# One Strassen level on two of the four chunks of a spatial mixing matmul, with z2 stored by feature planes and the attention's output projection moved to the end

## The chip, the cores and the metric

The kernel runs on one core of one Trainium2 chip. The metric is the device time of one execution in microseconds (us). An execution is somewhat longer than the span of the profile, which begins with the first and ends with the last instruction or transfer that the profiler records.

## The reference

A token mixer over S = 2048 positions of width D = 512, all in float32. After a layer norm of `x`, two branches run and are joined:

```python
xn = _layernorm(x, axis=-1)
s = _A_ref(xn, A_wqkv, A_wo)        # 32 heads of 16; each position looks at 8 positions, 2 apart
g = _silu(_B_ref(xn, ...))
return x + s * g

# branch B
z = _gelu(jnp.einsum("bsd,df->bsf", x, w_in))
z1 = z[..., :Fh]                                   # Fh = 896
z2 = _layernorm(z[..., Fh:], axis=-1)
g = jnp.einsum("ts,bsf->btf", w_sp, z2) + b_sp[None, :, None]   # the spatial mixing, w_sp is 2048 x 2048
return jnp.einsum("bsf,fd->bsd", z1 * g, w_out)
```

The spatial mixing is the largest product: 2048 x 2048 times 2048 x 896.

## The kernel before

Every matmul operand is split in two parts, `hi` (rounded to the type fp32r that TensorE reads) and `lo` (the rest), and each product is three matmuls: hi by hi, hi by lo, lo by hi. ScalarE (ACT) makes the hi part with a copy, VectorE (DVE) makes the lo part with a subtraction (`split`, L155 and L156; with a scale for the spatial weights in `prep`, L139 and L140).

The work on TensorE (PE) stands in this order. First q, k and v for 16 tiles of 128 positions (`product`, `pair`, L344 to L364), which go to DRAM (`qkv_d`). Then z1 (L528 to L530), kept transposed, through a gelu to DRAM (`z1_d`). Then z2 (`z2_half`, L552 to L554) with its layer norm: statistics on DVE (L567, L568), small steps on GpSimd (POOL), the centred hi and lo parts by ACT and DVE (L571, L572) into the large resident buffer `BIG`. Then the spatial mixing in four chunks `c` of 512 output positions (L607 to L609): for each of 16 blocks `js` of input positions and each of 7 blocks `f` of features three matmuls of 128x512, so 336 per chunk, into 7 of the 8 PSUM banks. At the end of a chunk ACT copies the banks out (L629), DVE adds the bias (L636) and multiplies by z1 (`gated`, L585), and the result `ut` goes to DRAM (`g_d`); the last chunk stays on chip. In the end phase the projection `b` of the gated result (21 matmuls a tile) and the projection `s` of the attention (12 matmuls a tile) alternate tile by tile (`tail`, L652 to L654), then silu, product, residual and output.

The attention itself has no matmul. DVE does it (`attention`, L471 to L508) for 8 groups of heads, at the lowest priority, between DVE's other work; the outputs go to DRAM in `o_d` and come back in the end phase (`load_o`).

What sets the order: a scheduler lays all instructions of each engine in one fixed sequence before the run, with priorities from the order of the code; instructions in `pin` keep the order of the code. On the chip each engine works through its sequence in that order and waits at its head. PSUM has 8 banks in one pool (`mm`). Split weights have 8 buffers of each part (`whi`, `wlo`), loads of weights have 3 (`raw`); they are requested by SyncE's queue (SP) in the order of its sequence.

Of the kernel before, what the change touches and what calls it, by code (L numbers as in the profile page):

```python
# [16 lines left out]
P = 128  # L17
# [17 lines left out]
HALO = (W - 1) * DIL  # L35
PAD = 16
# [10 lines left out]
def kernel(  # L47
# [52 lines left out]

    def xn_at(j):
        o = (NT * 2 * (FH - D)) + j * 2 * D
        return BIG[:, o : o + D], BIG[:, o + D : o + 2 * D]

    def z2_at(j):
        o = j * 2 * FH
        return BIG[:, o : o + FH], BIG[:, o + FH : o + 2 * FH]

    def ut_at(c, f):
        o = c * 2 * FB * CT + f * 2 * CT  # L110
        return BIG[:, o : o + CT], BIG[:, o + CT : o + 2 * CT]
# [6 lines left out]

    def mm(name):
        return ps.tile([P, 512], F32, tag="mm", name=name, bufs=8)  # L120

    def fetch(src, n, name):
        raw = raws.tile([P, 512], F32, tag="raw", name=name + "r", bufs=3)
        pin(nc.sync.dma_start(raw[:, :n], src))
        return raw

    def prep(src, n, name, pool=None, scale=None, raw=None):
        if raw is None:
            raw = fetch(src, n, name)
        if pool is None:  # L130
            hi = wts.tile([P, 512], F32R, tag="whi", name=name + "h", bufs=8)
            lo = wts.tile([P, 512], F32R, tag="wlo", name=name + "l", bufs=8)
        else:
            hi = pool.tile([P, 512], F32R, tag=name + "h", name=name + "h")
            lo = pool.tile([P, 512], F32R, tag=name + "l", name=name + "l")
        if scale is None:
            split(hi[:, :n], lo[:, :n], raw[:, :n])
        else:
            nc.scalar.activation(hi[:, :n], raw[:, :n], AF.Copy, scale=scale)  # L139
            nc.vector.scalar_tensor_tensor(  # L140
                lo[:, :n], raw[:, :n], scale, hi[:, :n].bitcast(F32), op0=ALU.mult, op1=ALU.subtract
            )
        return hi, lo

    def rstd(mv):
        nc.vector.tensor_scalar(mv[:, 1:2], mv[:, 1:2], EPS, None, op0=ALU.add)
        nc.gpsimd.tensor_tensor(mv[:, 1:2], mv[:, 1:2], nhalf, op=ALU.pow)
# [6 lines left out]
    def split(hi, lo, src):  # L154
        pin(nc.scalar.activation(hi, src, AF.Copy))  # L155
        pin(nc.vector.tensor_tensor(lo, src, hi.bitcast(F32), op=ALU.subtract))  # L156

# [25 lines left out]
    def turned_x(j, xt):  # L183
        pt = mm(f"xt_{j}")
        for i in range(KB):
            pin(nc.tensor.transpose(pt[:, i * P : (i + 1) * P], xt[:, i * P : (i + 1) * P], ident))
        pin(nc.scalar.activation(xn_at(j)[0], pt, AF.Copy))
        return pt

    def low_x(j, pt):  # L190
        hi, lo = xn_at(j)
        pin(nc.vector.tensor_tensor(lo, pt, hi.bitcast(F32), op=ALU.subtract))
# [42 lines left out]
    def column_tile(j):  # L235
# [5 lines left out]
        pin(nc.scalar.activation(xn_at(j)[0], cols[j], AF.Copy))  # L241
# [10 lines left out]
    def opening(wg):  # L252
        def high(k):
            hi = wts.tile([P, 512], F32R, tag="whi", name=f"wqkv_0_{k}h", bufs=8)
            lo = wts.tile([P, 512], F32R, tag="wlo", name=f"wqkv_0_{k}l", bufs=8)
# [8 lines left out]
        def times(j, *kab):  # L264
            for k, a, b in kab:
                pin(nc.tensor.matmul(
                    first[j], xn_at(j)[a][:, k * P : (k + 1) * P], wg[k][b],
# [70 lines left out]
    def product(g, j, wg):  # L338
        xh, xl = xn_at(j)
        pq = mm(f"qkv_{g}_{j}")  # L340
        for k in range(KB):
            wh, wl = wg[k]
            c = slice(k * P, (k + 1) * P)
            nc.tensor.matmul(pq, xh[:, c], wh, start=k == 0, stop=False)  # L344
            nc.tensor.matmul(pq, xh[:, c], wl, start=False, stop=False)  # L345
            nc.tensor.matmul(pq, xl[:, c], wh, start=False, stop=k == KB - 1)  # L346
# [74 lines left out]
    for g in range(1, NG):  # L421
        for j in range(OPEN if g == 1 else 0, NT, 2):
            if g == 1 and j == NT // 2:
# [3 lines left out]
                rb = t2("rb", tag="tz", bufs=2)  # L427
# [13 lines left out]
    att = tc.tile_pool(name="att", bufs=1)  # L441
    ap_ = att.__enter__()
    NJ = 4
    at_priority = [LOW]

    def attention(sub):
# [49 lines left out]
        for j0 in range(0, NT, NJ):  # L496
# [9 lines left out]
            nc.vector.tensor_tensor(pr[:, 0], pr[:, 0], pr[:, 1], op=ALU.add)  # L506
            tt = ap_.tile([P, NJ * CS // Q, Q], F32, tag="tt", name=f"tt_{sub}_{j0}", bufs=2)
            nc.vector.transpose(tt.rearrange("p n q -> p (n q)"), pr[:, 0])  # L508
            for a in range(P // Q):
                dst = o_d[sub, j0 : j0 + NJ, :, a * Q : (a + 1) * Q]  # L510
                nc.sync.dma_start(
                    dst.rearrange("j (b c) q -> c (j b) q", c=Q), tt[a * Q : (a + 1) * Q]
# [7 lines left out]
    xall = BIG[:, NT * 2 * (FH - D) :].rearrange("p (c j a k t) -> p c a k j t", c=NC, j=JC, a=2, k=KB)  # L520
    for f in range(FB):
        wh, wl = prep(w_in1[:, f, :], KB * P, f"w1_{f}")
        for c in range(NC):
            pz = mm(f"z1_{f}_{c}")
            for k in range(KB):
                cc = slice(k * P, (k + 1) * P)
                xh, xl = xall[:, c, 0, k], xall[:, c, 1, k]
# [3 lines left out]
            zt = t2(f"z1t_{f}_{c}")  # L531
# [4 lines left out]
            nc.scalar.dma_start(z1_d[c, f], zt)  # L536
# [185 lines left out]
```

## Time and profile before

| | us |
|---|---|
| median of 3 runs (725.66 to 725.99) | 725.96 |
| the profiled execution | 725.2 |
| its span | 723.2 |
| PE busy in the span | 717.1 |
| DVE busy | 566.9 |
| ACT busy | 222.1 |
| POOL busy | 33.5 |
| DMA, share of 16 engines' span, both large queues | 39.1% and 10.9% |

Busy time is the time in which at least one instruction of the engine runs. Matmuls are pipelined: one lasts 389 ns in the profile, while the next begins long before it ends, so the distance between starts is what a matmul costs. Stages can be found by the lines named above: chunk 0 of the spatial mixing begins at about 295 us, and the end phase at about 600 us.

### The profile page before, as it was taken

Reading aid. Unit: us, or ns where it says so; the run is one execution under the profiler, and the core shown is the slowest. Engines: PE = TensorE matmul, PEld = TensorE weight load, DVE = VectorE, ACT = ScalarE, POOL = GpSimd, SP = SyncE. Lnnn points to the kernel's source line nnn. Section 1 sums busy time; section 2 is a strip of 40 time slices with the busy share of each in tenths; the row PEclk is TensorE's granted clock in tenths of the full one; section 3 lists DMA queues with packets and bytes.
Section 4 is the critical chain, followed back from the end, with each engine's and each line's share of the span. In section 5 each row is a group of like instructions: output and inputs, shape, how many; then the busy total and the mean of one; then the engine's idle time right before and its main releaser. Section 6 shows DMA issues by size and latency. Waiting matters only on the chain.

```text
span 723.2 us, 8807 instructions
## 1 busy us (share of the span) xinstructions
PE 717.1 (99%) x3224; PEld 599.1 (83%) x3224; DVE 566.9 (78%) x683; ACT 222.1 (31%) x341; POOL 33.5 (5%) x49
## 2 busy tenths in 40 slices
PE   8999999999999999999999999999999999999997
PEld 7888888888888889888888888888888888888886
DVE  6763699889989999999997999999999947432222
ACT  4443332342243345621231123111334234311210
POOL 3100000000001223300000000000000000000000
PEclk9999999999999999999999999999999999999999
DMA  8776874674562210352457334744368547523221
GB/s 283 237 203 183 296 245 125 189 247 142 185 219 67 63 59 26 95 166 71 148 149 249 130 83 130 258 150 132 92 222 276 150 125 204 161 88 118 86 73 44
DMA packets 111178, 111.55 MB, mean 154 GB/s; under 512 B 40736, under 2 KB 74784, under 8 KB 111136
## 3 DMA queue, kind: packets, MB, share of 16 engines
q1 hardware_dynamic: 79120, 85.43, 39.1%
q10 hardware_dynamic: 32016, 25.56, 10.9%
q8 instruction: 25, 0.41, 0.2%
q14 instruction: 17, 0.14, 0.1%
HBM read 77.07 MB, written 33.90 MB: 153 GB/s over the span
## 4 chain that ended last, share of the span: by engine, by line
PE 93%; DMA 3%; DVE 3%; SPq 1%; issue 0%; POOL 0%; ACT 0%; DVEq 0%
PE g L609 14%; PE g L607 14%; PE g L608 14%; PE qkv L346 4%; PE qkv L344 4%; PE qkv L345 4%; PE z L554 4%; PE z L553 4%; PE z L552 4%; PE b L654 4%; PE b L653 4%; PE z L530 4%; PE z L528 4%; PE b L652 4%; PE z L529 4%; PE s L654 2%
## 5 line engine op out<-in xcount | busy, mean ns | idle before, releaser
L471 DVE TENSOR_TENSOR pr<-k,q 128x2048 f32<-128x2048 f32 x32 | 73.2, 2287 | 1.5 <-DMA q<-qkv_d 1.1
L498 DVE TENSOR_TENSOR pv<-v,lg 128x2048 f32<-128x2048 f32 x32 | 73.3, 2289 | 0.9
L474 DVE TENSOR_REDUCE lg<-pr 128x128 f32<-128x2048 f32 x32 | 72.9, 2280 | 0.5
L666 DVE TENSOR_TENSOR sg<-s,sg 128x512 f32<-128x512 f32 (+1 forms) x17 | 11.2, 659 | 71.5 <-PE s L654 71.5
L504 DVE TENSOR_TENSOR pv<-pv 128x1024 f32<-128x1024 f32 x32 | 39.0, 1220 | 0.5
L364 ACT ACTIVATE stage<-qkv 128x512 f32<-128x512 f32 x36 | 21.4, 596 | 50.8 <-PE qkv L346 50.7
L661 ACT ACTIVATE sg<-b 128x512 f32<-128x512 f32 x16 | 9.6, 597 | 60.7 <-PE b L654 56.9
L585 DVE TENSOR_TENSOR gt<-gt,zl 128x512 f32<-128x512 f32 x28 | 18.9, 687 | 11.1 <-DMA zl<-z_d 11.1
L554 PE MATMUL z<-w_0h,BIG 128*128 128x512 f32 x64 | 25.0, 391 | 0.0
L553 PE MATMUL z<-w_0l,BIG 128*128 128x512 f32 x64 | 25.0, 391 | 0.0
L552 PE MATMUL z<-w_0h,BIG 128*128 128x512 f32 x64 | 24.9, 389 | 0.0
L155 ACT ACTIVATE BIG<-ul 128x512 fp32r<-128x512 f32 x21 | 13.2, 631 | 32.6 <-PE g L608 19.3
L505 DVE TENSOR_TENSOR pv<-pv 128x512 f32<-128x512 f32 x32 | 22.0, 688 | 0.6
L238 DVE TENSOR_TENSOR xT<-xT,mr 128x512 f32<-128x512 f32 x20 | 13.7, 687 | 10.9 <-DMA mr<-mv_d 6.1
L554 PE MATMUL z<-w_1h,BIG 128*128 128x384 f32 x64 | 21.5, 336 | 0.0
L552 PE MATMUL z<-w_1h,BIG 128*128 128x384 f32 x64 | 21.5, 335 | 0.0
L553 PE MATMUL z<-w_1l,BIG 128*128 128x384 f32 x64 | 21.4, 335 | 0.0
L569 POOL TENSOR_TENSOR nmz<-mvz,mone 128x1 f32<-128x1 f32 x16 | 10.0, 627 | 222.5 <-DVE mvz L568 219.7
L571 ACT ACTIVATE BIG<-zt,nmz 128x896 fp32r<-128x896 f32 x16 | 16.6, 1041 | 10.8 <-POOL nmz L569 10.8
L572 DVE SCALAR_TENSOR_TENSOR BIG<-zt,mvz,BIG 128x896 fp32r<-128x896 f32 x16 | 18.2, 1143 | 2.2 <-ACT BIG L571 2.0
L567 DVE BATCH_NORM_STATS2 zst<-zt 128x6 f32<-128x448 f32 x32 | 18.7, 607 | 0.4 <-ACT zt L555 0.2
L555 ACT ACTIVATE zt<-z 128x512 f32<-128x512 f32 (+1 forms) x24 | 12.6, 539 | 19.8 <-PE z L554 19.6
(396 smaller groups left out, 2113.0 us busy)
## 6 DMA issues: line engine op xcount, KB each, us to landing
qkv_d<-stage ACTq DMA_DIRECT2D x24, 512.0 KB
x<-in_x SPq DMA_DIRECT2D x32, 256.0 KB
k<-qkv_d SPq DMA_DIRECT2D x8, 960.0 KB
v<-qkv_d SPq DMA_DIRECT2D x8, 960.0 KB
z_d<-z1t ACTq DMA_DIRECT2D x28, 256.0 KB
zl<-z_d SPq DMA_DIRECT2D x28, 256.0 KB
ul<-g_d SPq DMA_DIRECT2D x21, 256.0 KB
g_d<-gt ACTq DMA_DIRECT2D x9, 512.0 KB
```

Source lines behind the costliest of these rows:

```text
L344: nc.tensor.matmul(pq, xh[:, c], wh, start=k == 0, stop=False)
L471: nc.vector.tensor_tensor(pr, taps(kw, j0), qb.unsqueeze(1).to_broadcast([P, W, NJ * CS]), op=ALU.mult)
L474: nc.vector.tensor_reduce(lg[:, :, j0 * HS : (j0 + NJ) * HS], pr.rearrange("p w (i d) -> p w i d", d=DH), axis=AX.X, op=ALU.add,)
L498: nc.vector.tensor_tensor(pr.rearrange("p w (i d) -> p w i d", d=DH), taps(vw, j0).rearrange("p w (i d) -> p w i d", d=DH), lg[:, :, j0 * ...
L504: nc.vector.tensor_tensor(pr[:, 0:4], pr[:, 0:4], pr[:, 4:8], op=ALU.add)
L552: nc.tensor.matmul(pz, xh[:, c], wh, start=k == 0, stop=False)
L553: nc.tensor.matmul(pz, xh[:, c], wl, start=False, stop=False)
L554: nc.tensor.matmul(pz, xl[:, c], wh, start=False, stop=k == KB - 1)
L607: nc.tensor.matmul(pg[f], zh[:, ff], wh, start=js == 0, stop=False)
L608: nc.tensor.matmul(pg[f], zh[:, ff], wl, start=False, stop=False)
L609: nc.tensor.matmul(pg[f], zl[:, ff], wh, start=False, stop=js == NT - 1)
L654: nc.tensor.matmul(pp[:, cols], lo, wh, start=False, stop=k == n - 1)
```

## The change

**Products.** Chunks 2 and 3 are mixed directly as before, and first. Chunks 0 and 1 together form a two by two block product: the output positions are the two chunks, the input positions the two halves of 8 blocks, and of the 7 feature blocks six are taken as two halves of three. One level of Strassen's method (the form with 7 products and shared sums) does these: seven block products of 8 position blocks by 3 feature blocks, so 7 x 8 x 3 x 3 = 504 matmuls. The odd feature block (`ODD`, number 3) is mixed directly: 2 x 16 x 3 = 96 matmuls. Together 600 where the two chunks had 672. Each product is a call of `block_product` (p1, p2, q6, q7, q5, q3, q4).

**Sums.** The sums of weight blocks (`block_sums`, four subtractions or additions of 128x512 for each of 8 blocks) are made by DVE from the loaded weights and stored in DRAM (`sums_d`), during z1 and the direct chunks. The sums of z2 blocks (`combine`, four of 128x384 for each of 8 pairs of tiles) are made by DVE in the z2 stage and stored (`t_d`); they come back in pairs (`operand`) into the place of feature blocks 4 to 6 in `BIG`, are split there, and are replaced four times (T2, T3, T1, T4). The products are combined by `minus` on DVE, and a product that follows into the same bank adds onto it.

**Bias and evictions.** ACT writes the bias into a PSUM bank (`seed`) and the matmuls add to it, for six blocks of chunk 3 and for the products p1 and q7 and the odd blocks. Where the bank was seeded, DVE multiplies by z1 straight from the bank; in chunk 2 and for the first block of chunk 3 DVE adds the bias from the bank into a buffer first. ACT copies no bank of the direct chunks any more.

**z2.** `BIG` is laid out by feature planes (`planes`). The variance is now applied to z2 itself and no longer to the spatial weights: GpSimd takes four small steps a tile in place of two, ACT normalises (`z2_normal`) and then splits. The tiles are made in pairs (i, 8 + i).

**Tail.** All 16 tiles of `b` come first and are stored (`b_d`), then all 16 of `s`; in the last stage `b`, `x` and the attention's tiles come back in pairs of tiles, paced by dependencies on splits (`fetch_pair`), and the output leaves in pairs. `o_d` is laid out so that loads and stores have longer rows.

**Buffers.** A pool of 8 wide buffers `t4` takes the place of several small ones, PSUM banks and weight buffers are taken in a fixed turn, and there are 4 `raw` buffers.

```diff
-    for c in range(NC):
-        pg = [mm(f"g_{c}_{f}") for f in range(FB)]
-        for js in range(NT):
-            wh, wl = prep(w_sp[c, js], CT, f"wsp_{c}_{js}", scale=mvz[:, js, 1:2])
...
-            if c < NC - 1:
-                nc.scalar.activation(gt, pg[f], AF.Copy)
...
+    def seed(key, name, src, scale=1.0):
+        banks[key] = mm(name)
+        nc.scalar.activation(banks[key], src, AF.Copy, scale=scale)
+        seeds.add(key)
+
+    for c in (2, 3):
+        for n, js in enumerate(order):
+            w = spatial.get((c, js)) or spatial_block(c, js)
             for f in range(FB):
...
+                if (c, f) not in seeds:
+                    gt = gts[:, f - f0]
+                    nc.vector.tensor_tensor(gt, src, bb[:, c - 2], op=ALU.add)
+                    src = gt
+                nc.vector.tensor_tensor(zt, src, zt, op=ALU.mult)
+                if c == 2 and f < FB - 1:
+                    seed((3, f + 1), f"g_3_{f + 1}", bb[:, 1])
...
+    def block_product(name, key, z, w, odd=None, start=True, steps=()):
+        for n, s0 in enumerate(range(0, HT, 2)):
+            pair_ = [(s, prep(w(s), CT, f"{name}_{s}")) for s in (s0, s0 + 1)]
+            for f in range(3):
+                for s, wp in pair_:
+                    three(
+                        banks[key, f], z(s, f), wp, start and s == 0, s == HT - 1, not start
+                    )
+            if odd:
+                for s, wp in pair_:
+                    three(banks["o", odd[0]], odd[1](s), wp, False, s == HT - 1, True)
+            for do in steps[n] if steps else ():
+                do()
...
+    def block_sums(i):
...
+        for out_, a, b in (
+            (low[:, 1], top[:, 1], low[:, 1]),
+            (top[:, 1], top[:, 0], top[:, 1]),
+            (top[:, 0], top[:, 0], low[:, 1]),
+            (low[:, 0], top[:, 0], low[:, 0]),
+        ):
+            nc.vector.tensor_tensor(out_, a, b, op=ALU.add)
...
+    rows_of = [c * JC + jj for c in (0, 2, 3, 1) for jj in range(JC)]
+    groups = [rows_of[i] // NJ for i in range(0, NT, NJ)]
+    fetched = {0: fetch_pair(0)}
+    os_ = [load_o(groups[0], k, slots[2, 0] + k) for k in range(KB)]
+    fetched[2] = fetch_pair(2, arrived[groups[0]])
```

Three places show how instructions move. In the rows stand the line, the operation, output <- inputs, and the size; buffer numbers follow the names.

**First place: PE where the second direct chunk begins.** Before, on PE, from the last matmuls of chunk 0 (bank g_6) to chunk 1 (banks g_0, g_1); `wsp_0h` is the hi part of the weights of position block 0:

```order
L608 MATMUL g_6_2890<-wsp_15l,BIG 128x512
L609 MATMUL g_6_2890<-wsp_15h,BIG 128x512
L607 MATMUL g_0_3365<-wsp_0h,BIG 128x512
L608 MATMUL g_0_3365<-wsp_0l,BIG 128x512
L609 MATMUL g_0_3365<-wsp_0h,BIG 128x512
L607 MATMUL g_0_3365<-wsp_1h,BIG 128x512
L607 MATMUL g_1_3366<-wsp_0h,BIG 128x512
```

With the change, from chunk 2 to chunk 3 (two rows before these also write g_0):

```order
L695 MATMUL g_0_3245<-wsp_0h,BIG 128x512
L695 MATMUL g_0_3245<-wsp_8h,BIG 128x512
L695 MATMUL g_0_3245<-wsp_8l,BIG 128x512
L695 MATMUL g_0_3245<-wsp_8h,BIG 128x512
L695 MATMUL g_0_3245<-wsp_1h,BIG 128x512
L695 MATMUL g_0_3245<-wsp_1l,BIG 128x512
L695 MATMUL g_0_3245<-wsp_1h,BIG 128x512
L695 MATMUL g_0_3245<-wsp_9h,BIG 128x512
L695 MATMUL g_0_3245<-wsp_9l,BIG 128x512
L695 MATMUL g_0_3245<-wsp_9h,BIG 128x512
L695 MATMUL g_1_3460<-wsp_0h,BIG 128x512
```

Before, 4 matmuls of the free bank g_0 stood ahead of the first one that needs a bank of the chunk before; now 12 do.

**Second place: who empties those banks.** Before, on ACT, the copies stand in one row behind the splits of weights:

```order
L139 ACTIVATE wsp_5h<-wsp_5r,mvz 128x512
L139 ACTIVATE wsp_6h<-wsp_6r,mvz 128x512
L629 ACTIVATE gt_0_3325<-g_0_2884 128x512
L629 ACTIVATE gt_0_3325<-g_1_2885 128x512
L629 ACTIVATE gt_2_3328<-g_2_2886 128x512
L629 ACTIVATE gt_2_3328<-g_3_2887 128x512
L629 ACTIVATE gt_4_3331<-g_4_2888 128x512
L629 ACTIVATE gt_4_3331<-g_5_2889 128x512
```

With the change, on DVE, at the end of chunk 2 (L739 empties a bank, L741 multiplies by z1, L184 splits a weight, L503 and L506 are attention):

```order
L503 TENSOR_TENSOR pr_4_1460<-k_1451,q_1450 128x2048
L506 TENSOR_REDUCE lg_1456<-pr_4_1460 128x8x16
L739 TENSOR_TENSOR gt_0_3457<-g_0_2987,bb_2985 128x512
L184 TENSOR_TENSOR wsp_3l<-wsp_3r,wsp_3h 128x512
L739 TENSOR_TENSOR gt_0_3457<-g_1_2988,bb_2985 128x512
L503 TENSOR_TENSOR pr_8_1463<-k_1451,q_1450 128x2048
L739 TENSOR_TENSOR gt_2_3469<-g_2_2989,bb_2985 128x512
L741 TENSOR_TENSOR zl_0_3455<-gt_0_3457,zl_0_3455 128x512
L739 TENSOR_TENSOR gt_2_3469<-g_3_2990,bb_2985 128x512
L739 TENSOR_TENSOR gt_4_3481<-g_4_2991,bb_2985 128x512
```

The emptying of the banks has moved from ACT to DVE, and attention stands between the evictions.

**Third place: SP in the last stage.** Before, on SP, in the middle of the end phase (`ol` attention, `x` residual, `out` results; tile by tile):

```order
L668 DMA out<-sg_5133 128x512
L659 DMA x_6_5327<-in_x 128x512
L591 DMA ol_5347<-o_d 64x4x128
L591 DMA ol_5396<-o_d 64x4x128
L668 DMA out<-sg_5182 128x512
```

With the change, around the start of `s` (`sg` is `b` coming back, `tt` an attention output that is stored):

```order
L548 DMA o_d<-tt_12_1732 32x2x128 x4
L932 DMA sg_5616<-b_d 128x1024
L933 DMA x_4_5617<-in_x 128x1024
L932 DMA sg_5651<-b_d 128x1024
L678 DMA ol_0_5784<-o_d 64x512 x2
L933 DMA x_6_5652<-in_x 128x1024
L678 DMA ol_3_5707<-o_d 64x512
L678 DMA ol_1_5791<-o_d 64x512
L971 DMA out<-sg_5560 128x1024
```

The transfers of a tile, spread over 33 matmuls of `b` and `s` before, have moved behind the attention's last store and beside the 12 matmuls a tile of `s`, in pieces twice as large, and `b` itself has joined them.

More of the change, by code (lines that the diff above doesn't have):

```diff
@@ L541 @@
         (k, h): prep(w_in2[:, k, HALF[h]], WID[h], f"w2_{k}_{h}")
+        for h in range(2)
         for k in range(KB)
-        for h in range(2)
     }
@@ new lines, in upper, with lower, turned, fresh @@
+    def upper(s, f):
+        return z2_block(s, f)
+    def lower(s, f):
+        return z2_block(HT + s, f)
+    def turned(s, f):
+        return z2_block(s, FB - 3 + f)
+    def fresh(key, name):
+        for f in range(3):
+            banks[key, f] = mm(f"{name}_{f}")
+    def odd_upper(s):
+        return z2_block(s, ODD)
+    def odd_lower(s):
+        return z2_block(HT + s, ODD)
+    def gated(c, f, src, zt):
+        nc.vector.tensor_tensor(zt, src, zt, op=ALU.mult)
+        split(*ut_at(c, f), zt)
@@ new lines @@
+    T1, T2, T3, T4 = [[later(operand, i, h, s0) for s0 in range(0, HT, 2)] for i, h in ((0, 0), (1, 1), (1, 0), (0, 1))]
+    block_product("p1", "p", upper, lambda s: w_sp[0, s], (0, odd_upper), start=False)
+    ya, yb = t4("ya"), t4("yb")
+    oq = t4("oq")
+    yv, o1 = [ya[:, 0], ya[:, 1], yb[:, 0]], oq[:, 0]
+    with urgent(400):
+        for f in range(3):
+            nc.scalar.activation(yv[f], banks["p", f], AF.Copy)
+        nc.scalar.activation(o1, banks["o", 0], AF.Copy)
+    nc.vector.tensor_tensor(b01[:, 1], b01[:, 0], b01[:, 1], op=ALU.add)
@@ new lines @@
+    block_product(
+        "p2", "p", lower, lambda s: w_sp[0, HT + s], (0, odd_lower), start=False,
+        steps=([], [T2[0]], [T2[1]], [T2[2]]),
+    )
+    fresh("q", "q6")
+    block_product(
+        "q6", "q", turned, lambda s: sums_d[0, s, :, 0],
+        steps=(
+            [T2[3], later(upper_first, 0)],
+            [T3[0], later(upper_first, 2)],
+            [T3[1], later(late, 2, 0, 2)],
+            [T3[2], later(late, 2, 2, 2)],
+        ),
+    )
+    for f in range(3):
+        minus(yv[f], banks["q", f], yv[f])
@@ new lines @@
+    for f in range(3):
+        seed(("q", f), f"q7_{f}", b01[:, 1], -1.0)
+    seed(("o", 1), "o2", b01[:, 1])
+    block_product(
+        "q7", "q", turned, lambda s: sums_d[0, s, :, 1], (1, odd_upper), start=False,
+        steps=([T3[3]], [T1[0]], [T1[1]], [T1[2], later(late, 2, 4, 1)]),
+    )
+    va, vb = t4("va"), t4("vb")
+    vv = [va[:, 0], vb[:, 0], yb[:, 1]]
+    for f in range(3):
+        minus(vv[f], yv[f], banks["q", f])
+    fresh("q", "q5")
+    block_product(
+        "q5", "q", turned, lambda s: sums_d[1, s, :, 1],
+        steps=([T1[3]], [later(late, 2, 5, 2)], [], []),
+    )
@@ new lines @@
+    qv = [va[:, 1], vb[:, 1], oq[:, 1]]
+    with urgent(400):
+        for f in range(3):
+            nc.scalar.activation(qv[f], banks["q", f], AF.Copy)
+    block_product(
+        "q3", "q", lambda s, f: z2_block(HT + s, FB - 3 + f), lambda s: sums_d[1, s, :, 0], start=False,
+        steps=([T4[0], later(lower_last, 4, 2)], [T4[1], later(lower_last, 6, 1)], [T4[2]], [T4[3]]),
+    )
+    fresh("q4", "q4")
+    block_product(
+        "q4", "q4", turned, lambda s: w_sp[1, HT + s], (1, odd_lower), start=True,
+        steps=(
+            [later(upper_last, 4, 2)],
+            [later(upper_last, 6, 1)],
+            [later(late, 3, 0, 2)],
+            [later(late, 3, 2, 1)],
+        ),
+    )
@@ L647, in proj @@
+    for f in range(3):
+        banks["q", f] = banks["q4", f]
+    wout = [prep(w_out[:, f, :], D, f"wout_{f}") for f in range(FB)]
+    lower_first(0)
+    lower_first(2)
+    late(3, 3, 2)
+    late(3, 5, 2)
     def proj(n, src, w, name, cols=slice(0, D)):
```

432 lines of the change are left out of this document (284 added, 148 removed).

## Prediction

> **What bounds the kernel now.** I read the busy times first, then the waits of PE, then the chain that ended last, then the stages. Engine, busy us (share of the span) and instructions; the wait rows give who waited for whom, us in total, times, longest; the chain row gives shares of the span.
>
> ```profile
> PE 717.1 (99%) x3224; PEld 599.1 (83%) x3224; DVE 566.9 (78%) x683; ACT 222.1 (31%) x341; POOL 33.5 (5%) x49
> ...
> PEclk9999999999999999999999999999999999999999
> ```
> ```profile
> PE warm L247 <- POOL ident masks.py:199: 1.4, 1, 1.4
> PE xt L186 <- DVE mvx L171: 0.5, 1, 0.5
> PE qkv L266 <- ACT BIG L187: 0.2, 1, 0.2
> ```
> ```profile
> PE 93%; DMA 3%; DVE 3%; SPq 1%; issue 0%; POOL 0%; ACT 0%; DVEq 0%
> ```
>
> PE is busy 99% of the span at the full granted clock, its recorded waits sum to 2.1 us, all in the opening, and 93% of the chain is PE. So a matmul that goes shortens the run by its own spacing, unless a wait takes its place. The spacing comes from one group whose first instance is the first feature block of chunk 0 and whose last is the seventh of chunk 3 (duration min/median/max, first and last start):
>
> ```profile
> L607 PE MATMUL g<-wsp_7h,BIG x28: 389/389/389, 328.0 to 560.6; 128*128 128x512 f32 x28
> ```
>
> Between the two lie three chunks of 336 and 6 x 3 = 18 matmuls, 1026 in 232.6 us: **0.2267 us each**, across chunk ends too.
>
> **What the change takes from PE.** Chunks 0 and 1 took 672 matmuls and take 600; PE's sequence shrinks by the same 72. 72 x 0.2267 = 16.3 us. The profiled execution took 725.2 us (2.0 around its span, which I keep), so matmuls alone give **708.9**. The median of the runs shown is 0.8 higher, so a result may lie that much above the sum.
>
> The Trainium skill, "TensorE: Matmul & The Clock Gate", section "Back-to-back issue gap", gives about 131 ns as the sustained spacing for 512 columns. By that the 72 matmuls would be worth 9.4 us and the sum 715.8; the trace, 226.7 ns over 1026 matmuls, decides against it.
>
> **What is added, and what hides it.** The critical question is DVE, which fills its time with attention. A row of stages gives the stretch, its length, busy us (instructions) of PE, weight loads, DVE, ACT and POOL, the granted clock, the DMA share and GB/s; group rows follow.
>
> ```profile
> 371.00:524.00 153.00, 153.00 (x677) 126.73 (x676) 142.68 (x137) 33.02 (x50) 0.00 (x0) 1.00 0.52 156
> ```
> ```profile
> L498 DVE TENSOR_TENSOR pv<-v,lg 128x2048 f32<-128x2048 f32 x32 | 73.3, 2289 | 0.9
> ...
> L504 DVE TENSOR_TENSOR pv<-pv 128x1024 f32<-128x1024 f32 x32 | 39.0, 1220 | 0.5
> ...
> L585 DVE TENSOR_TENSOR gt<-gt,zl 128x512 f32<-128x512 f32 x28 | 18.9, 687 | 11.1 <-DMA zl<-z_d 11.1
> ...
> L572 DVE SCALAR_TENSOR_TENSOR BIG<-zt,mvz,BIG 128x896 fp32r<-128x896 f32 x16 | 18.2, 1143 | 2.2 <-ACT BIG L571 2.0
> ...
> L508 DVE STREAM_TRANSPOSE tt<-pv 128x256 f32<-128x256 f32 x32 | 14.2, 444 | 0.9
> L506 DVE TENSOR_TENSOR pv<-pv 128x256 f32<-128x256 f32 x32 | 13.4, 420 | 0.7
> ...
> L491 DVE TENSOR_REDUCE sm<-lg 128x64 f32<-128x512 f32 x8 | 8.6, 1077 | 7.4 <-ACT lg L489 7.3
> ...
> L492 DVE RECIPROCAL sm<-sm 128x64 f32<-128x64 f32 x8 | 4.4, 551 | 0.2
> ```
>
> The first row is chunks 1 and 2: DVE 142.7 busy of 153 us, yet PE ran without a break, since 8 split weights were ahead of it and ACT emptied the banks. In the group rows the last numbers are busy us, mean ns | idle before, and whom for.
>
> Now the DVE sequence with the change, from the first bank of chunk 2 that it empties to the first subtraction behind product q4; PE's matmuls between those points are chunk 3 and seven products, 336 + 600 = 936, or 212.2 us. DVE has there 30 attention instructions of 2048 elements (x 2.289 = 68.7 us), 9 of 1024 (11.0), 9 of 256 (3.8), 9 transposes (4.0), 6 reductions of 512 (6.4), 3 reciprocals (1.7); 159 instructions of 512 elements, attention's among them (x 0.687 = 109.2); and 16 splits of operands of 768, a size that the trace lacks: between the rows for 512 and 896 elements, 0.687 and 1.143, I take 0.99, on the line between them (15.8). The sum is 220.6, 8.4 more than PE. But durations overlap (start, duration):
>
> ```profile
> 321.03 0.74 DVE L140 SCALAR_TENSOR_TENSOR wsp_12l<-wsp_12r,mvz,wsp_12h 128x512 fp32r<-128x512 f32 x1
> 321.69 1.22 DVE L504 TENSOR_TENSOR pv<-pv 128x1024 f32<-128x1024 f32 x1
> 322.94 0.69 DVE L505 TENSOR_TENSOR pv<-pv 128x512 f32<-128x512 f32 x1
> ```
>
> The split leaves its last 0.08 us to the next instruction; one that reads the result of the one before leaves none. With an estimated 100 independent ones, 8 us come back: 212.6. Then DVE's own waits, in the 153 us of above:
>
> ```profile
> DVE gt L585 <- DMA zl<-z_d: 4.4, 2, 3.6
> DVE wsp_10l L140 <- ACT wsp_10h L139: 1.4, 1, 1.4
> ```
>
> The 4.4 for z1 may recur, since z1 is still fetched shortly before use: 4.4 x 212 / 153 = 6.1. The wait for ACT arises where DVE is early, so I leave it out. DVE then needs 218.7 us, a lag of 6.5 on PE. It meets PE where DVE empties banks, which ACT did before:
>
> ```profile
> L629 ACT ACTIVATE gt<-g 128x512 f32<-128x512 f32 x21 | 12.6, 599 | 1.5
> ```
>
> An eviction (0.69), a seed by ACT (0.60) and one attention instruction that stands in front (2.29) make 3.6 us from a bank's last matmul to its next first one. PE has meanwhile the 18 matmuls of the other six blocks (4.1) and 12 on the free bank (2.7), 6.8. So 3.2 of a lag is covered, and 6.5 costs PE about **3 us**, once, since DVE catches up while PE waits. The bounds are 0 (overlap and cover hold, no wait recurs) and 8.4 + 6.1 = 14.5 (nothing overlaps, every wait recurs, no cover). I take 3, nearer the lower end, because the quoted starts show the overlap and chunks 1 and 2 left DVE 10 us idle.
>
> Other additions are free where their cover is named. In the z2 stage a pair of tiles takes PE 9.67 us (pieces of the chain, start and us, one pair apart); the stage's busy times and its POOL and ACT rows follow:
>
> ```profile
> 237.06 0.24 PE z L553
> ...
> 246.73 0.24 PE z L553
> ```
> ```profile
> 220.00:295.00 75.00, 75.00 (x376) 67.62 (x375) 71.60 (x105) 35.98 (x52) 19.50 (x28) 1.00 0.16 48
> ```
> ```profile
> L571 ACT ACTIVATE BIG<-zt,nmz 128x896 fp32r<-128x896 f32 x16 | 16.6, 1041 | 10.8 <-POOL nmz L569 10.8
> ...
> L147 POOL TENSOR_TENSOR mvz<-mvz,nhalf 128x1 f32<-128x1 f32 x16 | 13.9, 869 | 19.2 <-DVE mvz L146 19.1
> ```
>
> Eight POOL steps a pair at 0.87 are 7.0 us, less than a pair's time, and z2 is normalised one pair later, so the matmuls of the next pair hide them; uncovered, the 7.0 would be paid once, at the stage's end. The z2 sums, four of 384 elements a pair (between 0.42 and 0.69 each, at most 2.8 us), take DVE's time from attention, its filler; ACT, half idle in that row, takes a second pass of 1.04 a tile. Eight lots of weight sums, 22 us of DVE (32 x 0.687), also push attention back. That matters only if attention is late for `s`: from q4's first subtraction to the split of the last attention tile of the first `s` group, DVE has 65.5 us by the same rows (13 of 2048 elements, 33 of 512, 5 each of 1024, 256 and transposes, 3 small ones), PE 18 + 336 matmuls, 80.3 us. So 15 us hide it, at no cost; without that cover a late pass is paid in full.
>
> **The tail.** `s` alone takes 16 x 12 x 0.2267 = 43.5 us. The order puts behind the last `b` the loads of six pairs (2 x 0.52 MB each, 6.3 MB), the last attention group and a rest (1.2) and eight stores (4.2): 11.7 MB, 269 GB/s. What the engines moved when full (the last two numbers: DMA share, GB/s):
>
> ```profile
> 18.00:24.00 6.00, 6.00 (x31) 4.76 (x30) 4.37 (x12) 2.51 (x5) 1.10 (x2) 1.00 1.08 382
> 378.00:384.00 6.00, 6.00 (x28) 4.97 (x27) 5.91 (x7) 0.73 (x1) 0.00 (x0) 1.00 1.05 299
> 606.00:612.00 6.00, 6.00 (x28) 4.99 (x27) 4.41 (x8) 3.03 (x4) 0.00 (x0) 1.00 1.01 285
> ```
>
> At 285 to 382 the traffic needs 31 to 41 us of the 43.5, so it fits, with little to spare at the lower rate. SP issues in order: behind the first output, which waits for DVE, stand the attention tiles of the last group and the loads of later pairs. I take **1 us**, between 0 and 8; 8 is one more pass of a pair (1.57 MB at 285 GB/s, 5.5) and 2.5 of latency, an estimate from these rows. The end itself stays: last product and sum of half a tile on DVE, then the store.
>
> Sum: 725.2 - 16.3 + 3 + 1 = **712.9**.
>
> **Rivals.**
>
> *DVE sets the pace in the products.* For it: 220.6 against 212.2 us, and DVE in order. Against it: the overlap above. Its price is the upper bound, 14.5: 708.9 + 14.5 = 723.4, and anything from 716 on belongs here. Chance 0.15.
>
> *The last stage is short of data.* For it: 269 GB/s against 285. Against it: eight banks let PE run 8 tiles ahead, so only the end counts. 708.9 + 8 = 717. Chance 0.10.
>
> *Every seam waits (slower).* There are nine places where a stage takes over banks: chunk 2 to 3, chunk 3 to p1, six between the products, and q4 to `b`. If at each the eviction, the seed and the attention instruction, 3.6 us, came on top and not beside, 9 x 3.6 = 32.4 would go on: 741.3. It decides from 16.3 / 9 = 1.8 us a seam. Against it: most products use banks that were emptied a product (16 us or more) earlier, and PE's rows show other work placed there. Chance 0.08. The Trainium skill, "TensorE: Matmul & The Clock Gate", sections "Why this matters for your kernels" and "What's actually happening", speaks for this side: PE gaps over about 3 us bring the array back to half clock for a window of some 3.4 us. Here the longest recorded wait is 1.4 us and the granted clock stays in its top tenth, so no run shows it yet; two such gaps would cost an estimated 1.7 us each, and the sum would be 716.3.
>
> *No change.* Both the DVE bound and the tail bound come in part: the gain of 16.3 is eaten to within 1.4 us. Chance 0.04. That the matmuls are not saved at all is ruled out by the sequence of PE.
>
> **How the numbers follow.** The forecast, 0.63, has its own range of 708 to 716: matmuls alone less about 1 for scatter, and both terms at twice or more. For 8 in 10 I add the tail rival and most of DVE's: 708.0 to 721.5; what is left out is DVE's upper end, no change and slower. Faster by over 0.2% (under 724.5; about what a measurement of this kernel can tell) is 0.63 + 0.15 + 0.10 = 0.88; same 0.04; slower 0.08.
>
> **What would show it.** PE with 72 fewer matmuls at 0.227 us, its waits 4 to 8 us in sum, named after DVE and ACT at the seams of chunk 3 and p1; DVE over 95% busy from chunk 2 to q4; the granted clock unchanged; DMA near full in the last 43 us while PE does not wait. I am wrong if PE's spacing in the products is longer (the operand layout), if PE waits inside products for weights (the queue of SP), or if `s` starts late (attention).

## The result, and the profile after

| | us |
|---|---|
| median before, beside it on the same chip (4 runs, 725.44 to 725.99) | 725.81 |
| median with the change (4 runs, 708.18 to 709.00) | 708.38 |
| ratio | 0.9762, 95% interval 0.9745 to 0.9779 |
| forecast | 712.9 (708.0 to 721.5) |
| matmuls alone, the forecast without its two added terms | 708.9 |
| profiled execution with the change, and its span | 708.39, 706.6 |

The change is worth 17.4 us. The forecast's direction and range held, the range by 0.4 us at its lower end; the single number was 4.5 us too high, and the time is that of the matmuls alone. The first lines of the profile after, again the busy times, the granted clock and the chain of waits:

```profile
PE 700.7 (99%) x3152; PEld 585.4 (83%) x3152; DVE 619.2 (88%) x770; ACT 260.9 (37%) x403; POOL 41.8 (6%) x81
...
PEclk9999999999999999999999999999999999999999
...
PE 98%; DMA 1%; DVE 0%; SPq 0%; issue 0%
```

PE has 72 matmuls fewer and is 16.4 us less busy, while DVE is 52 us busier. The waits of PE (who for whom, us, times, longest):

```profile
PE warm L276 <- POOL ident masks.py:199: 1.3, 1, 1.3
PE xt L215 <- DVE mvx L200: 0.4, 1, 0.4
PE xt L215 <- DVE x L208: 0.3, 1, 0.3
PE qkv L294 <- ACT BIG L216: 0.2, 1, 0.2
```

They sum to 2.2 us, all in the opening, as before: no seam, no product and nothing in `s` made PE wait. Two stages, from the end of chunk 2 to the end of the products, and the stage `s` (length, then busy us of PE, weight loads, DVE, ACT, POOL, clock, DMA share, GB/s):

```profile
371.00:583.00 212.00, 212.00 (x937) 175.51 (x937) 205.47 (x245) 83.00 (x135) 0.00 (x0) 1.00 0.69 230
660.00:706.60 46.60, 42.99 (x201) 35.88 (x200) 26.14 (x36) 12.16 (x15) 0.00 (x0) 0.99 0.88 289
```

DVE is 97% busy in the first and PE does not notice. What DVE itself waited for there, the two longest, and the group of the operand splits (busy us, mean ns):

```profile
DVE p_6l L184 <- ACT p_6h L183: 1.4, 1, 1.4
DVE p_3l L184 <- ACT p_3h L183: 0.9, 1, 0.9
```
```profile
L184 DVE TENSOR_TENSOR BIG<-tr,BIG 128x768 fp32r<-128x768 f32 x16 | 15.1, 951 | 0.0
```

No wait for z1 is left. The seam of chunk 2 and chunk 3, DVE, then ACT, then PE (start, duration; `[idle before <-releaser]`):

```profile
366.99 2.29 DVE L506 TENSOR_REDUCE lg<-pr 128x128 f32<-128x2048 f32 x1
369.19 0.68 DVE L739 TENSOR_TENSOR gt<-g,bb 128x512 f32<-128x512 f32 x1
369.79 0.68 DVE L184 TENSOR_TENSOR wsp_3l<-wsp_3r,wsp_3h 128x512 fp32r<-128x512 f32 x1
370.39 0.69 DVE L739 TENSOR_TENSOR gt<-g,bb 128x512 f32<-128x512 f32 x1
```
```profile
369.91 0.60 ACT L714 ACTIVATE g<-bb 128x512 f32<-128x512 f32 x1 [2.95 <-DVE gt L739]
```
```profile
373.33 0.39 PE L695 MATMUL g<-wsp_9h,BIG 128*128 128x512 f32 x1
373.56 0.39 PE L695 MATMUL g<-wsp_0h,BIG 128*128 128x512 f32 x1
```

An attention instruction stands ahead of the first eviction, as the forecast had it. The eviction starts at 369.19, the bias is in the bank at 370.51, and PE comes to that bank at 373.56, one matmul spacing behind its predecessor: 3.05 us were left over. The DVE rows also show independent instructions of 512 elements that last 0.68 and start 0.60 apart.

### The profile page after: what moved, and what is told of

It reads as the page before. It is cut to its first block, busy times and chain, and to the rows that moved or that the text cites. A ratio compares the mean times of both kernels' runs of the same rounds, so it can differ in the third digit from the quotient of the medians.

```text
span 706.6 us, 8920 instructions
## 1 busy us (share of the span) xinstructions
PE 700.7 (99%) x3152; PEld 585.4 (83%) x3152; DVE 619.2 (88%) x770; ACT 260.9 (37%) x403; POOL 41.8 (6%) x81
## 4 chain that ended last, share of the span: by engine, by line
PE 98%; DMA 1%; DVE 0%; SPq 0%; issue 0%
PE g L695 22%; PE q L695 12%; PE p L695 6%; PE qkv L371 6%; PE qkv L373 6%; PE qkv L372 6%; PE z L608 4%; PE z L607 4%; PE z L606 4%; PE z L580 4%; PE b L911 4%; PE z L578 4%; PE b L910 4%; PE b L912 4%; PE z L579 4%; PE s L911 2%
## 5 line engine op out<-in xcount | busy, mean ns | idle before, releaser
L503 DVE TENSOR_TENSOR pr<-k,q 128x2048 f32<-128x2048 f32 x32 | 73.2, 2286 | 1.9 <-DMA q<-qkv_d 1.5
L506 DVE TENSOR_REDUCE lg<-pr 128x128 f32<-128x2048 f32 x32 | 73.0, 2281 | 0.4
L921 ACT ACTIVATE bt<-b 128x512 f32<-128x512 f32 x16 | 9.4, 597 | 41.5 <-PE b L912 41.5
L627 ACT ACTIVATE zt<-zt,nmz,mvz 128x896 f32<-128x896 f32 x16 | 17.9, 1134 | 17.6 <-POOL nmz L623 17.3
L587 ACT ACTIVATE z1t<-z 128x512 f32<-128x512 f32 x21 | 12.5, 594 | 21.8 <-PE z L580 21.8
L620 POOL TENSOR_TENSOR nmz<-mvz,mone 128x1 f32<-128x1 f32 x16 | 5.0, 315 | 234.8 <-DVE mvz L619 234.7
L184 DVE TENSOR_TENSOR BIG<-zt,BIG 128x896 fp32r<-128x896 f32 x16 | 17.1, 1079 | 1.1 <-ACT BIG L183 1.1
L609 ACT ACTIVATE zt<-z 128x512 f32<-128x512 f32 (+1 forms) x24 | 12.8, 535 | 13.4 <-PE z L608 12.1
L373 PE MATMUL qkv<-wqkv_0h,BIG 128*128 128x512 f32 x43 | 16.7, 389 | 0.0
```

The source lines that it names most:

```text
L373: nc.tensor.matmul(pq, xl[:, k], wh, start=False, stop=k == KB - 1)
L503: nc.vector.tensor_tensor(pr, taps(kw, j0), qb.unsqueeze(1).to_broadcast([P, W, NJ * CS]), op=ALU.mult)
L506: nc.vector.tensor_reduce(lg[:, :, j0 * HS : (j0 + NJ) * HS], pr.rearrange("p w (i d) -> p w i d", d=DH), axis=AX.X, op=ALU.add,)
```

## The experiments

Each time stands beside runs of the kernel before on the same chip (medians 725.3 to 725.6, and 725.8 in the table above). Ratios are to the kernel before. Differences in us to the changed kernel's 708.38 compare different chips, so some tenths of them may be the chip.

**72 matmuls more in the changed kernel.**

```diff
                 for s, wp in pair_:
+                    if name != "q4":
+                        three(banks["o", odd[0]], odd[1](s), wp, False, False, True)
                     three(banks["o", odd[0]], odd[1](s), wp, False, s == HT - 1, True)
```

> The changed kernel with 72 matmuls more: the odd feature block's three matmuls are done twice in p1, p2 and q7 (3 x 8 x 3 = 72), so that the mixing has as many matmuls as before the change. That block's sums come out doubled in part. Theory (the gain is the matmul count alone, and every other part of the change costs nothing): 708.4 + 72 x 0.2267 = 724.7, within 0.7 of the kernel before, PE waits as short as in the changed kernel. Rival (part of the 16.3 us was eaten by DVE at the seams and in the products, which more PE time would hide): 724.7 less that part, 721 to 723, since DVE gets 16 us more. Second rival (the other edits, larger transfers, fewer evictions, bring time of their own): under 724 too, but with PE's idle time in the opening or at stage borders shorter than before.

725.36 us, ratio 0.9997 (0.9988 to 1.0006). The matmul count explains the whole gain, within the 0.7 us allowed; all else that the change adds and takes cancels to less than that.

**72 matmuls fewer in the kernel before.**

```diff
-                nc.tensor.matmul(pg[f], zl[:, ff], wh, start=False, stop=js == NT - 1)
+                if not (c == 1 and 0 < js < 13 and f < 6):
+                    nc.tensor.matmul(pg[f], zl[:, ff], wh, start=False, stop=js == NT - 1)
```

> The kernel before the change with 72 of the lo by hi matmuls of chunk 1 left out (position blocks 1 to 12, feature blocks 0 to 5), nothing else; that chunk's result is less exact. Theory (0.2267 us a matmul wherever it goes): 725.8 - 16.3 = 709.5. Rival (a matmul's price is 0.131 us): 716.4. If this kernel comes out at the time of the changed one, Strassen's whole apparatus costs what it hides, nothing; if it comes out lower by 2 us or more, the apparatus costs the difference.

722.96 us, ratio 0.9972 (0.9958 to 0.9987): 2.6 us instead of 16.3, against the theory and the rival. The waits of PE and its busy time, and when DVE finished the last of the 32 attention outputs (first and last start), here and, in the second fence for that, in the kernel before:

```profile
PE s L653 <- ACT oh L155: 5.1, 1, 5.1
PE b L653 <- ACT wout_4h L155: 1.9, 1, 1.9
PE b L654 <- DVE wout_0l L156: 1.7, 1, 1.7
```
```profile
PE 705.7 (98%) x3152; PEld 587.5 (82%) x3152; DVE 566.3 (79%) x683; ACT 222.7 (31%) x341; POOL 33.1 (5%) x49
...
L508 DVE STREAM_TRANSPOSE tt<-pv x32: 432/446/448, 113.0 to 577.6; 128x256 f32<-128x256 f32 x32
```
```profile
L508 DVE STREAM_TRANSPOSE tt<-pv x32: 433/445/447, 112.8 to 578.7; 128x256 f32<-128x256 f32 x32
```

The attention ends within 1.1 us of where it did, though PE comes 16 us earlier. In this kernel the output weights `wout` take the buffers that the attention gives back (the pool `fin` opens behind `att`), so the end phase cannot be fed before. PE waits 8.7 us for it. And PE's busy time is 705.7, not 717.1 - 16.3 = 700.8: 4.9 us go to slower matmuls, 4.2 of them between 583.2 and 616.2 us, where the waits are (88 matmuls, 24.16 us busy, where 19.95 would do), mostly at half pace behind the waits (rows of one such stretch in the last section). 16.3 - 8.7 - 4.9 = 2.7 is what was measured.

**The same, with less attention.** A new theory, so a test of its own:

```diff
-            nc.vector.tensor_tensor(pr[:, 0:4], pr[:, 0:4], pr[:, 4:8], op=ALU.add)
```

> The kernel before the change, with the same 72 matmuls left out as in the run of before, and in the attention also without the first of the three adds that sum the eight taps (32 DVE instructions of 128x1024, 1.22 us each, 39 us; four of eight taps are then missing). Theory, new since 16.3 us less of PE gave the old kernel only 2.6: there the attention had to end before the end phase's weights could be loaded (they reuse its buffers), it ended at 577 us whatever PE did, and PE waited 8.7 us and then ran at half speed for a while. With DVE 39 us lighter the attention ends long before, and the 72 matmuls come in full: 725.6 - 16.3 = 709.3 (708.5 to 710.5), PE without waits after the opening. Rival (PE is held by the loads of the end phase's weights themselves, or left-out matmuls are worth less): 715 to 723.

709.56 us, ratio 0.9779 (0.9764 to 0.9794), as the theory said. The last attention output is turned (transposed, to be stored) at 520.6 us there, and PE has no wait behind the opening; its busy time is the expected 700.8 within half a microsecond:

```profile
PE 701.3 (99%) x3152; PEld 585.9 (83%) x3152; DVE 528.8 (75%) x651; ACT 221.3 (31%) x341; POOL 34.5 (5%) x49
```

So in the kernel before, the attention stood right behind PE as the next bound, hidden because PE never waited. A cut on PE alone would have brought 2.6 us there. The change also puts `s` behind all of `b`, and with that moves the attention's due time later (its last output in the changed kernel starts to be turned at 658.2 us). That the later due time is what lets the gain through in the changed kernel follows from these times; undoing only this order wasn't tried.

**No arithmetic in the weight sums.**

```diff
-            nc.vector.tensor_tensor(out_, a, b, op=ALU.add)
+            pass
```

> The changed kernel without the arithmetic of the weight sums (32 DVE instructions of 128x512, about 20 us of DVE, left out; loads and stores stay, so the products use unsummed weights). Theory (DVE's work is hidden, PE sets the time): 708.4, within 0.7. Rival (DVE at 97% between 371 and 583 us holds PE back a little everywhere): 2 to 5 us faster, since attention gets ahead by 20 us before the products begin.

708.52 us, ratio 0.9764 (0.9749 to 0.9778): no gain, though DVE is 17.8 us less busy (601.4 against 619.2). DVE's 97% costs nothing as it stands.

**168 matmuls fewer in the products, with the full and with the lighter attention.**

```diff
...
-                        banks[key, f], z(s, f), wp, start and s == 0, s == HT - 1, not start
+                        banks[key, f], z(s, f), wp, start and s == 0, s == HT - 1, not start,
+                        2 if name in ('p1', 'p2', 'q6', 'q7', 'q5', 'q3', 'q4') else 3,
```

(The last argument is the number of matmuls of the three that are done. The second kernel also lacks the attention's add of the edit above.)

> The changed kernel without the lo by hi matmul of the six block products' and the seventh's three feature blocks (7 x 8 x 3 = 168 fewer, 38.1 us of PE); DVE and ACT do all they did. The products are less exact. PE's stretch from 371 to 583 us shrinks from 212 to 174 us, DVE has 205.5 us of work in it, of which attention can move behind the products. Theory (PE sets the pace until DVE's idle 6.5 us, the cover of 3 at the seams and some 15 of attention's slack are used up, 25 us in all): 681 to 686, with PE waits for DVE. Rival A (DVE in its fixed order sets the pace, nothing of attention moves): gain 6.5 + 3 = 9.5, 699. Rival B (DVE has far more room than its busy share says): the full 38.1, 670.3.

> The changed kernel without 168 lo by hi matmuls of the products (38.1 us of PE), and without the first of the attention's three adds over taps (39 us of DVE). Theory (what took 32 of the 38 us away was DVE: the attention late for the last projection, operands and evictions late in the products): nearly all comes, 670.3 to 676. Rival (weights through ACT, SP's queue or the loads from DRAM are the limit at that pace): 685 or more, with PE waits for ACT's hi parts behind DMA.

702.48 us, ratio 0.9673 (0.9654 to 0.9693), and 684.90, ratio 0.9440 (0.9426 to 0.9455). Of 38.1 us the first brings 5.9, less than any rival gave, and the second 23.5, below the theory and just past the rival's edge. The longest waits of PE, first kernel, then second:

```profile
PE s L911 <- ACT o_3h L183: 5.8, 1, 5.8
PE q L695 <- ACT va L883: 2.3, 1, 2.3
PE q L695 <- DVE q_0l L184: 2.0, 1, 2.0
```
```profile
PE q L694 <- ACT q_0h L183: 4.2, 2, 3.8
PE q L694 <- ACT va L882: 3.0, 1, 3.0
PE q L694 <- DVE q_4l L184: 1.8, 2, 1.2
```

Of the 32.2 us missing in the first, 15.8 are PE's waits behind the opening, 7.7 slower matmuls (PE busy 670.3 us where 662.6 were due) and 8.5 the tail behind PE's last matmul (12.1 us, in the changed kernel 3.6). With less attention the wait in `s` is gone and 17.6 us come back; so DVE's load is the larger part. What is missing in the second, 14.6 us, is again waits (9.8) and slower matmuls (5.0). These waits stand mostly at the borders of the q products, for weights and for a bank that ACT copies out (`va`). Which of the two sets the pace there was not separated.

**More work for DVE in the products.** The lo part made twice, in two products, then in all seven:

```diff
...
         split(hi[:, :n], lo[:, :n], raw[:, :n])
+        if again:
+            pin(nc.vector.tensor_tensor(lo[:, :n], raw[:, :n], hi[:, :n].bitcast(F32), op=ALU.subtract))
...
```

> The changed kernel with the lo part of each weight of p1 and p2 made twice (16 more DVE instructions of 128x512, 10 to 11 us of DVE between 447 and 491 us; the result is the same). In the changed kernel DVE is busy 205.5 of the 212 us from 371 to 583, the first group of the last projection has its attention 11.5 us before PE comes to it, the third about 5 us. Theory (attention takes the delay, and the margin is that of the third group, 5 us, plus 2 to 3 of DVE's idle time): 710 to 715, waits of PE in the last projection, none at the seams. Rival A (as in the prediction, 15 us hide it): 708.4. Rival B (DVE in order holds PE back where it falls behind, in p1 and p2): 716 to 719, waits of PE inside p1 to q6.

> The changed kernel with the lo part of every weight of the seven products made twice (56 more DVE instructions of 128x512, 34 to 38 us; the result is the same). Theory (the margin of 8 to 9 us goes first, the rest is paid once, plus 2 to 4 us at half pace behind waits): 733 to 741. Rival A (attention moves into the 28 us that DVE idles behind 583 us, nearly all is hidden): 710 to 720. Rival B (every doubled split delays PE where it stands, also within the products): waits of PE within p1 and p2 already, 740 or more.

710.62 us (709.09 to 711.59), ratio 0.9792 (0.9776 to 0.9807), and 733.79, ratio 1.0111 (1.0096 to 1.0127), both in the theory's range. DVE is busy 8.1 and 31.4 us longer (627.3 and 650.6 against 619.2), less than was planned, and the medians rise by 2.2 and 25.4; so some 6 us are covered in both, and the rest is paid. With the small addition the place was guessed wrong: PE waits nowhere behind the opening. The end of the chain of the profiled execution shows where it goes instead (span 707.3, the fastest of the four runs, so it shows 0.7 of the 2.2 us):

```profile
690.88 9.05 DMA sg<-b_d
...
700.00 1.07 ACT sg L957
```

The attention ends 15 us later, the last load of `b` follows it, and the silu on it is late. With the large addition PE waits inside the products q5, q3 and q4, for lo parts that DVE owes, and only 0.9 us in `s`. In the rows `q_5l` is the lo part of the sixth weight block of any of the q products (waits in q5 and q3), `q_3l` that of the fourth (4.8 us in q4, 0.7 in q3). Waits inside products were what rival B had said, though for p1 and p2 and with 740 us or more:

```profile
PE q L697 <- DVE q_5l L169: 6.4, 2, 4.1
PE q L697 <- DVE q_3l L169: 5.5, 2, 4.8
```

All waits behind the opening sum to 15.8 us, and PE is busy 8.5 us longer (709.2 against 700.7) with the same matmuls: 24.3 of the 25.4.

**A long instruction at the seam of chunks 2 and 3.**

```diff
+                    if (c, f) == (2, 0):
+                        nc.vector.tensor_reduce(
+                            gt, src.unsqueeze(2).to_broadcast([P, CT, 24]), op=ALU.max, axis=AX.X
+                        )
                     nc.vector.tensor_tensor(gt, src, bb[:, c - 2], op=ALU.add)
```

> The changed kernel with one DVE instruction more at the seam of chunk 2 and chunk 3: a maximum over 24 copies of the first bank (128x12288 elements, by the attention's reduction of 2048 in 2.28 us about 13.7 us), ahead of the first eviction; the result is the same. The order then puts 22 matmuls on the free bank there and not 12. Theory (a delay at the seam is covered by the 18 matmuls of the other blocks and those on the free bank; slack measured 3.0 us, plus 10 matmuls, 2.3 us, makes 5.3): one PE wait of about 8.4 us at the seam, behind it some matmuls at half pace (1.5 us lost behind the wait of 5.1 us in the run of the old kernel with 72 matmuls fewer), and the attention 5 us later against PE, about its margin: 708.4 + 8.4 + 1.5 = 718, 716.5 to 721. Rival A (no cover at seams, what DVE loses PE loses): 722 or more. Rival B (cover of 10 us and more by the buffered weights): under 713.

719.31 us, ratio 0.9912 (0.9896 to 0.9929). The instruction, then what PE did:

```profile
369.69 12.95 DVE L740 TENSOR_REDUCE gt<-g 128x512 f32<-128x12288 f32 x1
```
```profile
375.34 0.39 PE L695 MATMUL g<-wsp_3h,BIG 128*128 128x512 f32 x1
383.29 0.80 PE L695 MATMUL g<-wsp_3l,BIG 128*128 128x512 f32 x1 [7.57 <-DVE wsp_3l L184]
383.89 0.63 PE L695 MATMUL g<-wsp_3h,BIG 128*128 128x512 f32 x1
384.31 0.63 PE L695 MATMUL g<-wsp_11h,BIG 128*128 128x512 f32 x1
384.74 0.63 PE L695 MATMUL g<-wsp_0h,BIG 128*128 128x512 f32 x1
...
387.73 0.59 PE L695 MATMUL g<-wsp_1l,BIG 128*128 128x512 f32 x1
388.15 0.41 PE L695 MATMUL g<-wsp_1h,BIG 128*128 128x512 f32 x1
388.40 0.40 PE L695 MATMUL g<-wsp_9h,BIG 128*128 128x512 f32 x1
```

12.95 us of delay, 7.6 us of wait: 5.35 covered, in number the theory's 5.3 (3.05 left over in the changed kernel and 10 matmuls more that the order put on the free bank). But PE waits there for `wsp_3l`, a weight's lo part that DVE makes behind the long instruction, and not for a bank, as the theory had it. The bank's own chain is hidden behind that wait. Its bias is written here:

```profile
383.88 0.60 ACT L714 ACTIVATE g<-bb 128x512 f32<-128x512 f32 x1 [11.73 <-DVE gt L743]
```

It is in at 384.48; without the wait for the weight PE would have come to the bank four spacings behind 375.34, at 376.25, and waited 8.2 us, near the theory's 8.4. So the price of a late eviction is near what was expected, and that 5.35 met 5.3 is in part luck. Behind the wait 12 starts, from 383.29 to 388.15, take 4.86 us for 11 spacings, 0.44 each, where 2.49 would do: 2.4 us more. 7.6 + 2.4 = 10.0 of the 10.9 measured.

**More traffic in the last stage.**

```diff
...
             nc.sync.dma_start(xt, rows_at(x, rows_of[i])),
+            nc.sync.dma_start(spare_d[i // 2], rows_at(x, rows_of[i])),
```

> The changed kernel with a copy of each pair of residual tiles from DRAM to another place in DRAM beside its load (8 of 0.52 MB, 6 of them behind the attention's last store, 3.1 MB; the result is the same). In the changed kernel the stage s had 11.7 MB of my count in 43.5 us, a DMA share of 0.88 at 289 GB/s. Theory (the last stage is near what the DMA engines carry): 14.8 MB at 289 to 305 GB/s are 49 to 51 us, so 713 to 717, with the last outputs late and PE waiting for attention tiles or banks in the last 30 us. Rival (the stage has room up to 345 to 380 GB/s, the rates seen elsewhere): 708.4 to 710, the rate in the last 46 us going up to 340.

713.01 us, ratio 0.9825 (0.9809 to 0.9841), the lower edge of the theory's range, though PE does not wait there as the theory had it. The last stage, and the last silu here and in the changed kernel:

```profile
660.00:706.60 46.60, 42.89 (x201) 35.84 (x199) 25.62 (x34) 13.18 (x17) 0.00 (x0) 0.99 0.98 341
```
```profile
703.65 1.06 ACT L957 ACTIVATE sg<-sg 128x1024 f32<-128x1024 f32 x1 [4.27 <-DMA sg<-b_d]
```
```profile
696.47 1.06 ACT L955 ACTIVATE sg<-sg 128x1024 f32<-128x1024 f32 x1 [2.99 <-DMA sg<-b_d]
```

The rate rose to 341 GB/s at a DMA share of 0.98, as the rival said, and yet the time rose by 4.6 us. PE ended as in the changed kernel; the last silu began 7.2 us later. Here 7.4 us lie between that silu and the end of the span (711.1), and 7.3 in the run with the lo parts of two products made twice. In the changed kernel 696.47 + 7.3 = 703.8 is 2.8 us before the end that PE sets, 706.6. So **2.8 us** is the room in the last stage: 7.2 - 2.8 = 4.4.

**A second cut of 72, and the same with earlier loads.** The first leaves out the lo by hi matmul in p2, q6 and q7; the second also has:

```diff
-            fetched[i + 4] = fetch_pair(i + 4, arrived[groups[min(i // NJ + 1, 3)]])
+            fetched[i + 4] = fetch_pair(i + 4, arrived[groups[i // NJ]])
```

> The changed kernel without the lo by hi matmul of the three feature blocks of p2, q6 and q7 (72 fewer, 16.3 us of PE; those products are less exact), DVE's work as it was: a second cut of the size that the change made. Theory (10 us more of DVE cost 2.2 us, so DVE has some 8 to 9 us in hand against PE; what goes beyond is waited for, and matmuls behind a wait run at half pace): gain 5 to 9 us, 699.5 to 703.5, with PE waits late in the program, for the attention. Rival A (PE alone sets the time): 692.1. Rival B (168 fewer gave only 5.9, so nothing is to be had): 705 to 708.4.

> The kernel of the run with 72 matmuls fewer in p2, q6 and q7 (less exact, as there), with the last stage's pairs of b and x paced one group of attention tiles earlier (pair i + 4 behind the group of pair i, where it stood behind the next group). In that run PE ended at 689.3 us and the span at 700.5: the last four pairs were requested together behind the last attention group (the last at 684.3), took 8.8 us to land, and silu, product and sum came after. Theory (what ate 10.7 of the 16.3 us was the chain attention's end, last attention load, four pairs at once, silu; two of the four pairs now go ahead of it): 693 to 697, the end of the span 2 to 5 us behind PE's. Rival (PE itself waits for attention, which is as late as before): 701 to 703, PE's end as before. Second rival (the earlier loads only push attention's loads back, since the DMA engines are full): 700 to 705.

702.83 us, ratio 0.9688 (0.9674 to 0.9702), 5.6 us gained, the theory's size, though the waits of PE for the attention that it named are only 1.3 us; and 704.87, ratio 0.9715 (0.9698 to 0.9731), a miss. In the first, PE's last matmul ends at 689.3, the span at 700.5; its chain near the end:

```profile
677.57 2.69 DMA ol<-o_d
680.28 0.64 ACT o_3h L183
...
684.32 8.83 DMA sg<-b_d
693.17 1.07 ACT sg L956
```

PE kept 13.7 of the 16.3 us, but the last attention tile, the loads of `b` behind it and the silu end the run: 693.17 + 7.3 = 700.5. The pacing was therefore suspected, wrongly: with the loads ahead, SP sends the attention's stores and loads later (the last output is turned at 669.4, before at 667.1), and the time fell into the second rival's range, though the DMA engines were not full (share 0.71 from 680 to 690 us). The last silu begins at 693.40, only 0.2 us later than in the first; what the last sums wait for is the last `x`, requested at 686.6 and in at 694.6:

```profile
686.63 7.99 DMA x<-in_x
```

As the rows read, the attention's end and SP's order bound this tail together; which of them weighs more stays open, and no better order was found.

## Why the prediction was right

The main term was right, and the two terms added to it, 4 us together, measured 0. The range held because its lower end was the matmuls alone less a little scatter, not because the added terms were sized well.

**72 x 0.2267 = 16.3.** Right, and shown twice: 72 matmuls more in the changed kernel cost 17.0 us (725.36 against 708.38), 72 fewer in the old kernel with DVE made light bring 16.0 (725.54 to 709.56). The 131 ns of the Trainium skill's "TensorE: Matmul & The Clock Gate", section "Back-to-back issue gap", would have made 9.4 of it; both runs speak against it for this stream.

**The DVE term, +3.** Mis-sized: it measured 0, since PE waits nowhere behind the opening. Attention does stand ahead of the evictions and DVE is 97% busy, but the lag of 6.5 us that the term is made of did not arise, and the waits of 4 to 8 us in sum at the seams, named as a sign, did not come. Two sizes were too dark. The 6.1 us of waits for z1 did not recur. The overlap of independent instructions was put at 8 us: the mean durations of the 248 instructions that DVE starts from 369.1 to 583 us sum to 226.6, and they keep it busy for 207.4 us, so it was 19. One size was too light: the durations sum to 226.6, where the forecast had 220.6. The cover at the seam was right: put at 3.2 us beyond one eviction, seed and attention instruction, it measured 3.05. The order makes part of that cover: it places the matmuls of the bank that is ready, 12 in the changed kernel and 22 with the long instruction at the seam.

**The additions at no cost.** The weight sums: 17.8 us less of DVE change nothing (708.52). The z2 stage: PE waits nowhere in it. The cover of 15 us for the attention was too hopeful as a measure of what DVE has in hand: the kernel covers some 6 us by the runs with more DVE work. What gives way first is not PE waiting for the first `s` group, as I argued; it is the very end, the last load of `b` behind the last attention tile.

**The tail term, +1.** Mis-sized: 0, with 2.8 us of room. The rival of a last stage short of data has its mechanism shown: 3.1 MB more in that stage cost 4.6 us. With 341 GB/s at a share of 0.98, it was not the 285 that I feared. The 2.5 us of latency in the upper bound can't be read from the rate rows that stand before it; a load of an attention tile took 2.69 us in the changed kernel with 72 matmuls fewer.

**Every seam waits.** Fell: not one seam did. That PE at a long wait loses more than the wait is shown, though (10.0 us for a wait of 7.6).

**What I had not seen** is in the kernel before: its own next bound, the attention, was close enough that 72 matmuls fewer would have brought only 2.6 us without a later due time for it. The forecast treated the move of `s` as a cost. That the gain rests on the room that this move gives is argued from these runs; no run took the move alone away.

## What to carry to other kernels

An engine at 99% without waits says what a cut on it is worth only until the next engine's deadline; find that deadline (here the end of a filler whose buffers the next phase needs) before counting on the cut, and test it by making the second engine lighter. An engine at 97% can cost nothing: look at who waits for it, not at its share. And price a wait of the bound engine with the slow matmuls behind it.

## What the runs showed of the hardware

Behind a wait PE runs at about half pace for some microseconds, and the granted clock is half there. For the wait of 7.6 us at the seam (a row of stages, the granted clock third from the end):

```profile
383.30:388.10 4.80, 4.80 (x11) 3.68 (x12) 4.80 (x6) 2.03 (x4) 0.00 (x0) 0.50 0.18 55
```

In the old kernel with 72 matmuls fewer it came behind a wait of only 1.9 us too, with a delay; a wait of 1.7 us that ended 7 us earlier, at 585.6, had been followed by no such stretch:

```profile
592.99 0.50 PE L653 MATMUL b<-wout_4h,BIG 128*128 128x512 f32 x1 [1.86 <-ACT wout_4h L155]
...
594.20 0.63 PE L654 MATMUL b<-wout_4l,BIG 128*128 128x512 f32 x1
594.63 0.63 PE L655 MATMUL b<-wout_4h,BIG 128*128 128x512 f32 x1
...
597.43 0.40 PE L654 MATMUL b<-wout_5l,BIG 128*128 128x512 f32 x1
```

Spacings of 0.43 us between 593.8 and 597.2, 3.4 us; behind the wait of 7.6 us it lasted 4.9. The Trainium skill, "TensorE: Matmul & The Clock Gate", section "What's actually happening", tells of a free-running window of some 3.4 us and two clocks, which fits the halved pace and the changing length and delay. Its section "Why this matters for your kernels" allows gaps up to about 3 us; here 1.9 us were enough.

One small step on GpSimd (128x1, negating the mean) took 0.315 us in the changed kernel (L620) and 0.627 before (L569), with the same operation and size. These are means of unlike instances, 0.18 to 0.60 us in the one kernel and 0.19 to 2.12 in the other. Spans on GpSimd are rough, and the cause stays open.
